# Attention feeding a gated MLP in fp32: S^T computed directly, the row maximum as a bias product, x^T divided by the sums

## The chip, the cores and the metric

The kernel runs on one core of a Trainium2 chip. The core has five engines that run side by side, each through its own list of instructions in order: TensorE (PE) multiplies, VectorE (DVE), ScalarE (ACT) and GpSimd (POOL) do elementwise work and reductions, and SyncE (SP) issues transfers. The metric is the device time of one execution in microseconds (us).

## The reference

The inputs are q, k and v of 8 batches, 8 heads, 576 positions and 64 numbers a head, and three weight matrices; all are fp32.

```python
scores = q @ k.transpose(0, 1, 3, 2) / sqrt(64)
mask = (pos[:, None] // 64) >= (pos[None, :] // 64)      # causal by blocks of 64
scores = where(mask, scores, -1e9)
attn = exp(scores - max(scores, -1))
attn = attn / (sum(attn, -1) + 1e-9)
x = (attn @ v) -> [8 * 576, 512]
out = (sigmoid(x @ w_gate) * (x @ w_val)) @ w_out        # 512 -> 1536 -> 512
```

The MLP's weights hold 1536 hidden features; the kernel counts them as 12 chunks of 128.

## The kernel before, in words

**Two ways of multiplying.** A product with fp32 operands is exact enough by itself, but it is issued as two matmul instructions and takes PE far longer for each column. The other way writes each operand as the sum of two parts of type float32r (names ending in H and L) and adds three products, H·H, L·H and H·L. The MLP uses the second way throughout.

**Pairs of heads.** The attention walks through 32 pairs p: 8 batches times 4 pairs of heads. Both heads of a pair lie in the 128 partitions, 64 rows each, and `tile_position` lets two matmuls with 64 rows work side by side. `load` (L206) fetches q, k and v of a pair, three pairs ahead for q and k. `prep(p)` (L266) turns k and q into K^T and Q^T: for p up to 4 by PE transposes and ACT, afterwards by DVE's 32x32 transposes (L274); for p from 8 on it also makes the H and L parts (L309 to L315), so that the scores of pairs 0 to 7 are fp32 products and those of pairs 8 to 31 are three float32r products, block 0 excepted.

**One pair's attention.** `attend(p)` (L331) returns a function that does one step of the pair at a time. Queries lie in blocks of 128 rows (3, 2, 1, 0) and a tail of 64; a block needs only the keys up to its own end.

- `s_blocks` and `s_tail` (L373, L393) compute S with queries on the partitions, write the mask with a DVE memset, take the negated row maximum with DVE (L367, L403), and let ACT write P = exp(S - max) with the row sums (L370, L405).
- `recip` and `norm` (L408, L412, with L480 for the tail) divide P by its sums: reciprocals and eight DVE multiplications, and one for the tail (ACT does three of these nine in pairs 4 to 7).
- `tr_main`, `tr_low`, `tr_tail` (L421, L430, L438) transpose P with 25 PE transposes, and ACT copies the results into G1 and G0 (L345).
- `av` (L449) computes x^T = V^T P^T in 14 fp32 products, 28 instructions; ACT copies it out of PSUM into `xT`.
- `finish` (L468) writes XH on ACT, stores `xT` to DRAM, and writes XL on POOL.

**The order.** The lists FIRST, REST and TURN (L30 to L34) give the steps of one iteration p of the loop at L777. Lower-case steps belong to pair p, and AV and TR to pair p-1; "k" and "q" run `prep(p+1)` and the loads of pair p+3. Behind each step stands a number of places, 12 in all in an iteration.

**The MLP between.** `mlp1` (L562) is a generator of PE work for the first 4 of the 12 chunks of hidden features: 192 matmuls of 288 columns (`hidden`, L121) and 48 or 60 of 512 columns (`out_mm`, L130) a batch. When a batch's fourth pair has had its AV, its generator is chained. At each place the loop deals about five of its matmuls (L799 to L811): they come behind the attention matmuls that were issued three places before (AHEAD) and, in the later pairs, behind the run of attention matmuls just ended. The contraction runs over pairs of heads in order, so a matmul of the fourth pair comes tenth to twelfth of twelve. KEEP (L23) holds back 52 or 32 matmuls for the change from one batch to the next. The elementwise work between the two products (`glu`, L141) is on ACT (tanh, cast), DVE (product) and POOL (low part).

**Other work in the same time.** `convert` (L73) rebuilds fp32 weights for the MLP on DVE and ACT, one piece for each of the first iterations (CONV_PLAN, L25). In the last two iterations `early_work` begins to prepare the second part.

**The second part.** Behind the loop, from L821 on, the other 8 chunks of hidden features are computed by seven products for each 2x2 block of the matrices (`product`, L831; `out_block`, L886). The change does not touch it.

**PSUM.** `ps_a` has three tiles of two banks, which the attention takes in turn; `ps_m` has two tiles of one bank for the MLP and for the first transposes.

## Time and profile before

| | us |
|---|---|
| three runs | 1222.08, 1225.13, 1223.28 |
| median of them | 1223.28 |
| span of the profiled execution | 1223.3 |
| first attention matmul | 7.40 |
| first matmul of AV of pair 0, and of pair 3 | 31.29, 79.09 |
| two batches in the steady stretch (252.00 to 400.10) | 148.10 |
| AV of the last pair | 597.08 |
| first matmul of the second part | 656.40 |

The profiled execution's span is 1223.3 us, the median of the runs to the digit shown, so differences worked out in the span carry over to the time. The profile gives for each engine the time in which it was busy. PE's instructions overlap in part, and a PE that is shown busy all the time is still only as fast as its instructions follow one another; so the cost of a PE instruction is read here from the distance between the starts of two that follow each other, not from its own duration. A row of the timeline gives the start, the length of the merged stretch, the engine, line and operation, what is written and read, and how many instructions were merged.

### The profile page before, as it was taken

What the parts mean: (1) busy time and instruction counts of PE and PEld (TensorE: products, weight loads), DVE (VectorE), ACT (ScalarE), POOL (GpSimd) and SP (SyncE); (2) the same over time, 40 slices, a digit from 0 to 9 for tenths busy, and PEclk for the clock granted to TensorE, in tenths of its full rate; (3) what the DMA queues carried; (4) which work ended last, traced back from release to release, by engine and by line L of the source; (5) the groups of instructions that cost most, each with busy time, mean ns of one, the idle gap of its engine ahead of it and who ended that gap; (6) DMA issues with size and microseconds to landing.
All of it is one profiled execution on the core that took longest, in us unless ns stands there. A gap on an engine that the chain in (4) does not pass through costs nothing.

```text
span 1223.3 us, 20662 instructions
## 1 busy us (share of the span) xinstructions
PE 1171.9 (96%) x7421; PEld 1030.8 (84%) x7421; DVE 861.9 (70%) x1691; ACT 651.2 (53%) x1523; POOL 337.9 (28%) x409
## 2 busy tenths in 40 slices
PE   6889899999999999999999999999999999999996
PEld 4567678888888888889798899999999998998995
DVE  6888876577575875757898967857866755755742
ACT  5778766666665776756544544444444322422420
POOL 1113232223222332313401132132132152361441
PEclk8889999999999999999999999999999999999998
DMA  8543242423424333332343245145197154264243
GB/s 212 130 103 90 53 109 43 113 68 63 109 60 102 70 76 85 76 86 82 97 147 128 62 160 190 41 166 187 37 326 289 55 180 140 77 197 136 79 148 103
DMA packets 239125, 142.91 MB, mean 117 GB/s; under 512 B 183600, under 2 KB 204080, under 8 KB 238384
## 3 DMA queue, kind: packets, MB, share of 16 engines
q1 hardware_dynamic: 227968, 122.43, 35.7%
q10 hardware_dynamic: 11056, 19.17, 4.4%
q8 instruction: 59, 0.97, 0.3%
q14 instruction: 42, 0.34, 0.1%
HBM read 94.37 MB, written 47.19 MB: 116 GB/s over the span
## 4 chain that ended last, share of the span: by engine, by line
PE 74%; DVE 14%; DMA 4%; ACT 4%; issue 2%; SPq 1%; POOL 1%; POOLq 0%; DVEq 0%; ACTq 0%
PE b L838 23%; PE bank L242 11%; PE m L126 11%; PE m L896 9%; PE m L135 7%; PE b L896 5%; PE bank L245 4%; DMA pr<-part_d 2%; DVE P L419 2%; ACT P L370 2%; DVE XL L730 2%; PE bank L126 1%; DVE nm L367 1%; PE bank L135 1%; DVE KQ L274 1%
## 5 line engine op out<-in xcount | busy, mean ns | idle before, releaser
L838 PE MATMUL b<-XH,w 128*128 128x384 f32 x1344 | 349.9, 336 | 5.4 <-DVE v L874 2.7
L838 PEld LDWEIGHTS b<-XH,w 128*128 128x128 f32 x1344 | 243.7, 188 | 12.6 <-DVE v L874 6.6
L838 PE MATMUL b<-XL,w 128*128 128x384 f32 x672 | 223.7, 335 | 0.0
L370 ACT ACTIVATE P<-bank,nm 128x512 f32<-128x512 f32 (+3 forms) x256 | 132.9, 533 | 86.4 <-DVE nm L367 74.7
L838 PEld LDWEIGHTS b<-XL,w 128*128 128x128 f32 x672 | 126.1, 188 | 1.2
L896 PE MATMUL m<-wo,hH 128*128 128x512 f32 x384 | 124.9, 391 | 0.0
L345 ACT COPY G<-bank 128x768 f32<-128x768 f32 (+3 forms) x160 | 106.2, 700 | 27.4 <-PE bank L245 26.0
L367 DVE TENSOR_REDUCE nm<-bank 128x2 f32<-128x1024 f32 (+3 forms) x128 | 104.8, 819 | 8.2 <-ACT P L370 5.7
L126 PE MATMUL m<-XH,wv 128*128 128x288 f32 x448 | 104.8, 304 | 2.9 <-DVE h L147 2.9
L126 PE MATMUL m<-XH,wg 128*128 128x288 f32 x448 | 106.1, 305 | 0.6 <-ACT t L145 0.6
L153 POOL TENSOR_TENSOR hL<-h,hH 128x288 fp32r<-128x288 f32 (+1 forms) x56 | 49.0, 875 | 182.4 <-ACT hH L152 171.7
L242 PE MATMUL bank<-G,VS 128*64 128x320 f32 (+4 forms) x896 | 95.2, 364 | 0.0
L245 PE MATMUL bank<-ident,P 128*128 128x128 f32 x640 | 90.0, 280 | 4.1 <-DVE P L419 3.6
L911 POOL TENSOR_TENSOR pr<-pr,pr 128x512 f32<-128x512 f32 x36 | 48.2, 1342 | 162.7 <-DMA pr<-part_d 117.0
L419 DVE TENSOR_SCALAR P<-P,sm 128x256 f32<-128x256 f32 (+3 forms) x248 | 87.8, 414 | 1.7
L242 PEld LDWEIGHTS bank<-G,VS 128*64 128x64 f32 x896 | 56.4, 138 | 36.8 <-issue 4.1
L245 PEld LDWEIGHTS bank<-ident,P 128*128 128x128 f32 x640 | 76.7, 144 | 12.4 <-ACT wo L117 3.1
L861 ACT ACTIVATE g<-g 128x384 f32<-128x384 f32 x72 | 37.2, 524 | 87.2 <-DVE g L874 62.2
L896 PEld LDWEIGHTS m<-wo,hH 128*128 128x128 f32 x384 | 71.9, 188 | 13.8
L729 ACT CAST XH<-XB 128x1536 fp32r<-128x1536 f32 (+2 forms) x72 | 65.9, 939 | 29.3 <-DVE XB L727 22.5
L473 POOL TENSOR_TENSOR XL<-xT,XH 128x576 fp32r<-128x576 f32 x32 | 47.2, 1476 | 123.5 <-ACT XH L470 107.8
L126 PEld LDWEIGHTS m<-XH,wv 128*128 128x128 f32 x448 | 74.8, 188 | 6.2 <-DVE h L147 4.2
(176 smaller groups left out, 2543.6 us busy)
## 6 DMA issues: line engine op xcount, KB each, us to landing
pr<-part_d SPq DMA_DIRECT2D x72, 256.0 KB, 3.7
xT_d<-xT ACTq DMA_DIRECT2D x32, 288.0 KB, 2.8
XB<-xT_d SPq DMA_DIRECT2D x16, 576.0 KB, 5.5
part_d<-ost SPq DMA_DIRECT2D x36, 256.0 KB, 4.0
out_dram<-ost SPq DMA_DIRECT2D x36, 256.0 KB, 2.8
VS<-in_v_dram SPq DMA_DIRECT2D x64, 128.0 KB, 2.5
part_d<-ost ACTq DMA_DIRECT2D x32, 256.0 KB, 2.1
rqk<-in_k_dram SPq DMA_DIRECT2D x108, 72.0 KB, 2.6
```

The source lines that it names most:

```text
L126: mm = nc.tensor.matmul(ps, lhsT=lh, rhs=rh, start=(i == 0), stop=(i == n - 1))
L135: mm = nc.tensor.matmul(ps, lhsT=lh[:, f, t * P:(t + 1) * P], rhs=rh, start=(i == 0), stop=(i == n - 1))
L153: lower.tensor_sub(out=hL, in0=h2[:, cols], in1=hH.bitcast(F32))
L242: pe_last[:] = [nc.tensor.matmul(*args, **kw).ins]
L245: pe_last[:] = [nc.tensor.transpose(*args).ins]
L345: mark("ACT", nc.scalar.copy(out=dst, in_=src))
L367: mark("DVE", nc.vector.tensor_reduce(out=nm[:, c0:c0 + 2], in_=ps[:, :, c:c + n], axis=AX.X, op=ALU.max, negate=True))
L370: mark("ACT", nc.scalar.activation(out=Pi[:, h], in_=ps[:, h, c:c + n], func=AF.Exp, bias=nm[:, c0 + h:c0 + h + 1], accum_out=sm[:, c0 + h ...
L419: mark("DVE", nc.vector.tensor_scalar_mul(Pi[:, h], Pi[:, h], sm[:, c0 + h:c0 + h + 1]))
L729: nc.scalar.copy(out=XO[j][0][:, a:b], in_=x)
L838: mm = nc.tensor.matmul(ps, lhsT=lh, rhs=rh, start=(first and k == 0), stop=(k == n - 1), skip_group_check=not first)
L896: mm = nc.tensor.matmul(po[t], lhsT=lh[:, f, t * P:(t + 1) * P], rhs=rh, start=(half == 0 and i == 0), stop=(half == 1 and i == 5))
```

## The change

- **The maximum is found ahead.** A new step generator `scores(p+1)` runs in iteration p. It computes S of the next pair with one product of the H parts, sets the mask, and has DVE write the negated row maxima into `NM`. Its step "m" transposes `NM` with five PE transposes, and ACT copies the result into `MT`.
- **S^T directly.** `weights` in `attend(p)` computes S^T, keys on the partitions, in four chunks (CHUNKS): three float32r products and a fourth product, `BL` by `MT`, that adds the row maximum (negated) and, for the masked half of a block, a very large negative number. ACT writes `PT[t] = exp` of a whole chunk, both heads in one instruction, without a bias and without sums.
- **No transposes and no division of P.** The 25 transposes of a pair, their copies into G1 and G0, the accumulator reads, `recip` and `norm` go. AV reads `PT` instead of G1 and G0.
- **The sums.** `add_up` adds the chunks' rows on POOL into `acc`, five additions; behind AV, six fp32 products with a 128x32 tile of ones, in four groups of 32 columns of PE, sum over the keys into PSUM.
- **The division.** `finish` copies x^T out of PSUM as before. DVE transposes the sums, adds 1e-9, takes nine reciprocals a row and transposes them back; SP stores the 4x288 result in DRAM and loads it again with two transfers that repeat it over 64 partitions each; DVE multiplies `xT` by it. XH, the store and XL come behind that.
- **H and L parts for every pair.** `prep` makes them for all pairs, from PSUM for p up to 4, and now runs two pairs ahead.
- **The order.** One list ORDER takes the place of the three; the steps of a group are one run of PE instructions, and the MLP matmuls that are dealt stand behind a run. The loop begins at p = -1. The MLP of a batch is chained in the group "add", after 7 places, instead of at AV.
- **At the start** POOL writes `NM`, `ones` and the mask pattern `Z`, and PE transposes `Z` into `BL`. `VSs` has two buffers instead of three; the buffer for w_out's pieces moves to another pool.

The diff, cut to its core:

```diff
-FIRST = (("s3", 1), ("TR2", 1), ("k", 1), ("s2", 1), ("TRt", 1), ("q", 1), ("t", 1), ("TRl", 1), ("sl", 1), ("AV", 2),
-         ("tr3", 1))
-REST = (("s", 3), ("t", 1), ("AV", 2), ("tr3", 1), ("k", 0), ("tr2", 1), ("q", 0), ("trl", 2), ("trt", 2))
-TURN = (("s3", 1), ("TR2", 1), ("k", 0), ("s2", 1), ("TRt", 1), ("q", 0), ("t", 1), ("TRl", 1), ("sl", 1), ("AV", 1),
-        ("tr3", 1), ("tr2", 1), ("trl", 1), ("trt", 1))
-N_FIRST = 7
+ORDER = ((("av", "0"), 3), (("s0", "1", "s1"), 2), (("2", "s2", "3"), 2), (("add", "mlp", "k", "q", "v"), 0), (("st",), 1),
+         (("prep",), 1), (("sm",), 1), (("prep",), 2))
+MASK, MASKED = -1e9, -1e30
...
+        PT = [at.tile([P, 2, n], F32, name=f"PT{n_}") for n_, n in enumerate((512, 320, 448, 320))]
...
+            H, Lo = (at.tile([P, 2, S], F32R, name=f"KQ{e}", bufs=2) for e in "HL")
...
+            def halves(i, cols, src):
+                if i:
+                    mark("ACT", nc.scalar.mul(out=H[:, 1, cols], in_=src, mul=scale))
+                else:
+                    mark("ACT", nc.scalar.copy(out=H[:, 0, cols], in_=src))
+                yield
+                hi = H[:, i, cols].bitcast(F32)
+                if i:
+                    mark("DVE", nc.vector.scalar_tensor_tensor(out=Lo[:, 1, cols], in0=src, scalar=scale, in1=hi,
+                                                               op0=ALU.mult, op1=ALU.subtract))
+                else:
+                    mark("DVE", nc.vector.tensor_sub(out=Lo[:, 0, cols], in0=src, in1=hi))
...
+        def scores(p):
+            (H, _), QB, NM = KQS[p], QBs[p % 2], NMs[p % 2]
+            def top(i, src):
+                mark("DVE", nc.vector.tensor_reduce(out=NM[:, i, :, 0], in_=src, axis=AX.X, op=ALU.max, negate=True))
+            def blocks(group):
+                ps = two_banks()
+                o = 0
+                for i in group:
+                    n = P * (i + 1)
+                    for h in range(2):
+                        matmul(ps[:, h, o:o + n], lhsT=H[rows(h), 1, i * P:(i + 1) * P], rhs=H[rows(h), 0, :n],
+                               start=True, stop=True, tile_position=(64 * h, 0))
+                    o += n
+                if len(group) == 1:
+                    nc.vector.memset(ps[0:64, :, o - 64:o], MASK)
+                else:
+                    nc.vector.memset(ps[0:64, :, 2 * P:].rearrange("p h (i n) -> p h i n", i=2)[:, :, :, 64:], MASK)
+                o = 0
+                for i in group:
+                    n = P * (i + 1)
+                    top(i, ps[:, :, o:o + n])
+                    o += n
+            def tail():
+                ps = two_banks()
+                for half in range(2):
+                    matmul(ps[:, half, :288], lhsT=QB.rearrange("p h q -> p (h q)"),
+                           rhs=H[:, 0, 288 * half:288 * half + 288], start=True, stop=True)
+                mark("DVE", nc.vector.tensor_reduce(out=NM[:, 4, 0, 0:1], in_=ps[:, :, :288], axis=AX.XY, op=ALU.max,
+                                                    negate=True))
+                mark("DVE", nc.vector.tensor_copy(out=NM[:, 4, 1, 0:1], in_=NM[:, 4, 0, 0:1]))
+            def turn():
+                MT = at.tile([P, S], F32R, name="MT")
+                ps = two_banks()
+                for i in range(4):
+                    transpose(ps[:, 0, i * P:(i + 1) * P], NM[:, i].rearrange("p h x -> p (h x)"), ident)
+                transpose(ps[:, 1, :P], NM[:, 4].rearrange("p h x -> p (h x)"), ident)
+                mark("ACT", nc.scalar.copy(out=MT[:, :4 * P], in_=ps[:, 0]))
                 for h in range(2):
+                    mark("ACT", nc.scalar.copy(out=MT[rows(h), 4 * P:], in_=ps[rows(h), 1, 64 * h:64 * h + 64]))
+                state[p] = MT
+            return lambda what: {"0": lambda: blocks((3,)), "1": lambda: blocks((2, 0)), "2": lambda: blocks((1,)),
+                                 "t": tail, "m": turn}[what]()
+        CHUNKS = (((0, 256, 320), (3, 384, 192)), ((0, 0, 256), (4, 512, 64)), ((1, 128, 448),), ((2, 256, 320),))
...
+            H, Lo = KQS.pop(p)
+            MT, VS = state.pop(p), VSs[p % 2]
+            def weights(t):
                 ps = two_banks()
+                o = 0
+                for c, q0, w in CHUNKS[t]:
+                    k0 = c * P if c < 4 else S - P
+                    ops = [(x[:, 0, k0:k0 + P], y[:, 1, q0:q0 + w]) for x, y in ((H, H), (Lo, H), (H, Lo))]
+                    ops.append((BL[:, c], MT[:, q0:q0 + w]))
+                    for j, (x, y) in enumerate(ops):
+                        for h in range(2):
+                            matmul(ps[:, h, o:o + w], lhsT=x[rows(h)], rhs=y[rows(h)], start=(j == 0),
+                                   stop=(j == len(ops) - 1), tile_position=(64 * h, 0))
+                    o += w
+                mark("ACT", nc.scalar.activation(out=PT[t], in_=ps[:, :, :o], func=AF.Exp))
+            def add_up():
+                acc = at.tile([P, 2, S - P], F32, name="acc")
+                add = nc.gpsimd.tensor_add
+                add(out=acc[:, :, :P], in0=PT[1][:, :, P:2 * P], in1=PT[2][:, :, :P])
+                add(out=acc[:, :, P:], in0=PT[0][:, :, :320], in1=PT[2][:, :, P:])
+                add(out=acc[:, :, P:], in0=acc[:, :, P:], in1=PT[3])
+                add(out=acc[:, :, 2 * P:], in0=acc[:, :, 2 * P:], in1=PT[0][:, :, 320:])
+                add(out=acc[:, :, 3 * P:], in0=acc[:, :, 3 * P:], in1=PT[1][:, :, 2 * P:])
+                state[p] = acc
+            def values():
+                acc = state.pop(p)
                 pv = two_banks()
+                for i, pieces in enumerate((
+                        ((0, PT[0], 0, 0, 320), (1, PT[2], P, 0, 320), (2, PT[3], 0, 0, 320), (4, PT[1], 256, 256, 64),
+                         (3, PT[0], 320, P, 192)),
+                        ((0, PT[1], 0, 0, 256), (1, PT[2], 0, P, P)))):
+                    for j, (c, G, go, oo, w) in enumerate(pieces):
                         for h in range(2):
                             matmul(pv[rows(h), i, oo:oo + w], lhsT=VS[:, c, rows(h)], rhs=G[:, h, go:go + w],
                                    start=(j == 0), stop=(j == len(pieces) - 1), tile_position=(0, 64 * h))
+                us = two_banks()
+                for half, oo, G, go, w in ((0, 0, PT[1], 0, P), (1, 0, acc, 160, 288), (0, P, acc, 0, 160)):
+                    for h in range(2):
+                        r = 64 * h + 32 * half
+                        matmul(us[r:r + 32, 0, oo:oo + w], lhsT=ones, rhs=G[:, h, go:go + w], start=True, stop=True,
+                               tile_position=(0, r))
+                return pv, us
+            def finish(pv, us):
+                xT = at.tile([P, S], F32, name="xT", bufs=2)
+                T = at.tile([P, 288], F32, name="T")
+                r9 = at.tile([P, 9], F32, name="r9")
                 for i, (n, q0) in enumerate(((320, 256), (256, 0))):
+                    mark("ACT", nc.scalar.copy(out=xT[:, q0:q0 + n], in_=pv[:, i, :n]))
+                nc.vector.transpose(out=T, in_=us[:, 0, :288])
+                nc.vector.tensor_scalar_add(r9, T[:, ::32], 1e-9)
+                nc.vector.reciprocal(r9, r9)
+                mark("DVE", nc.vector.transpose(out=T.rearrange("p (b c) -> p b c", c=32),
+                                                in_=r9.unsqueeze(2).to_broadcast([P, 9, 32])))
+                r_d = dram.tile([4, 288], F32, name="r_d", bufs=2)
+                nc.sync.dma_start(out=r_d, in_=T[::32])
+                rb = at.tile([P, S], F32, name="rb")
+                for h in range(2):
+                    nc.sync.dma_start(out=rb[rows(h)],
+                                      in_=r_d[2 * h:2 * h + 2].rearrange("a n -> (a n)").partition_broadcast(64))
                 XH, XL = x_tiles(b)
+                nc.vector.tensor_mul(out=xT, in0=xT, in1=rb)
                 nc.scalar.copy(out=XH[:, hp], in_=xT)
+                nc.scalar.dma_start(out=xT_d[b, hp * P:(hp + 1) * P, :], in_=xT)
                 nc.gpsimd.tensor_sub(out=XL[:, hp], in0=xT, in1=XH[:, hp].bitcast(F32))
...
+        for c in range(5):
+            ps = mbank()
+            transpose(ps[:, :P], Z[:, c], ident)
+            nc.scalar.copy(out=BL[:, c], in_=ps[:, :P])
...
+        now = prev = None
+        for p in range(-1, n + 1):
+            if p >= 0:
+                early_work(p, 0)
+            prev, now = now, attend(p) if 0 <= p < n else None
+            nxt = scores(p + 1) if p + 1 < n else None
+            pr = prep(p + 2) if 0 <= p + 2 < n else iter(())
             tick = 0
...
+            for group, places in ORDER:
+                run_begins()
+                for what in group:
+                    if what == "av":
+                        if prev:
+                            prev("av")
+                    elif what == "mlp":
+                        if p > 0 and pairs[p - 1][1] == NP - 1:
+                            pb = pairs[p - 1][0]
+                            mlp = itertools.chain(mlp, mlp1(pb, mbank if p < n else bank))
+                            left += F1 * 48 * NC // 4 + 3 * F1 * (5 if pb % 2 else 4)
+                            rate = (left - KEEP[pb > 0]) / (4 * TICKS)
+                    elif what == "prep":
+                        next(pr, None)
+                    elif what in "kq":
+                        if 0 <= p and p + 3 < n:
+                            load(p + 3, what)
+                    elif what == "v":
+                        if 0 < p and p + 1 < n:
+                            load(p + 1, "v")
+                    elif what[0] == "s":
+                        if nxt:
+                            nxt(what[1])
+                    elif now:
+                        now(what)
+                run_ends()
...
```

More of the change, by code (lines that the diff above doesn't have):

```diff
@@ L247, in transpose, with run_begins, run_ends @@
                 behind(pe_last[0], hold[0])
+        def run_begins():
+            opening[:] = dealt[-1:]
+        def run_ends():
+            hold[:] = pe_last
         def two_banks():
@@ L750, in attn_glu_kernel @@
         load(1, "v")
-        load(2, "v")
-        prev = None
         mlp = iter(())
```

301 lines of the change are left out of this document (58 added, 243 removed).

## The prediction

> **What bounds the kernel now.** I read the page first, then busy time by stretch, then PE's timeline where PE is full, then the groups by line.
>
> ```profile
> PE 1171.9 (96%) x7421; PEld 1030.8 (84%) x7421; DVE 861.9 (70%) x1691; ACT 651.2 (53%) x1523; POOL 337.9 (28%) x409
> PE 74%; DVE 14%; DMA 4%; ACT 4%; issue 2%; SPq 1%; POOL 1%; POOLq 0%; DVEq 0%; ACTq 0%
> ```
>
> ```profile
> 7.40:75.00 67.60, 52.18 (x307) 33.27 (x308) 56.67 (x125) 48.87 (x135) 9.37 (x14) 0.87 0.65 154
> 75.00:105.00 30.00, 29.42 (x211) 22.50 (x209) 23.04 (x52) 23.71 (x60) 8.87 (x11) 0.96 0.40 90
> 105.00:174.00 69.00, 61.95 (x431) 49.58 (x431) 58.01 (x122) 51.12 (x135) 19.51 (x25) 0.98 0.33 79
> 252.00:400.10 148.10, 147.31 (x1143) 127.45 (x1144) 101.04 (x216) 100.77 (x275) 43.80 (x72) 1.00 0.36 81
> 548.20:700.00 151.80, 144.33 (x938) 128.98 (x938) 137.00 (x278) 80.07 (x179) 29.96 (x30) 0.99 0.31 99
> ```
>
> The columns are the stretch, its length, busy time of PE, PEld, DVE, ACT and POOL, the granted clock, the DMA share and GB/s. There are three regimes. From 252 to 400 PE is busy 147.3 of 148.1 us while DVE and ACT have a third free: there only PE's own work counts. From 7.4 to 75, before any MLP work exists, PE is idle for 15.4 us and DVE is busy 84%: the attention runs at the pace of DVE and its round trips. From 105 to 174 PE is idle for 7.1 us. The change takes work from ACT and DVE, which are not the bound where most of the pairs run; so its worth is PE's sum per pair, plus what becomes of the idle time at the start, plus new waits.
>
> **PE's work for a pair, steady.** Start distances give the prices.
>
> ```profile
> 400.04 2.93 PE L242 MATMUL bank<-G,VS 128*64 128x320 f32 x28
> 402.89 0.40 PE L126 MATMUL m<-XL,wg 128*128 128x288 f32 x1
> ...
> 404.07 0.29 PE L126 MATMUL m<-XH,wv 128*128 128x288 f32 x1
> 404.20 0.29 PE L126 MATMUL m<-XL,wv 128*128 128x288 f32 x1
> 404.33 1.03 PE L245 MATMUL bank<-ident,P 128*128 128x128 f32 x8
> 405.12 0.51 PE L126 MATMUL m<-XH,wv 128*128 128x288 f32 x2
> ...
> 411.14 0.50 PE L242 MATMUL bank<-KH,QH 64*128 64x512 f32 x2
> 411.47 0.40 PE L242 MATMUL bank<-KH,QL 64*128 64x512 f32 x2
> 411.70 0.40 PE L242 MATMUL bank<-KL,QH 64*128 64x512 f32 x2
> 411.94 0.34 PE L242 MATMUL bank<-KH,QH 64*128 64x384 f32 x2
> ...
> 412.59 0.28 PE L242 MATMUL bank<-KH,QL 64*128 64x256 f32 x2
> 412.70 0.28 PE L242 MATMUL bank<-KL,QH 64*128 64x256 f32 x2
> 412.82 0.39 PE L242 MATMUL bank<-KQ 64*128 64x128 f32 x4
> 413.14 0.53 PE L126 MATMUL m<-XH,wv 128*128 128x288 f32 x2
> ...
> 415.37 0.33 PE L242 MATMUL bank<-KH,QBH 128*128 128x288 f32 x1
> ...
> 416.20 0.30 PE L126 MATMUL m<-XH,wv 128*128 128x288 f32 x1
> ```
>
> ```profile
> 400.04:416.83 16.79, 9.65 (x61) 8.23 (x60) 1.00 0.35 72
> ```
>
> The last row counts the MLP's matmuls (L126) from one AV to the next: 60, and 0.13 us from start to start makes 8.0 us. The other 8.8 us of the 16.79 are attention: AV 2.85, transposes 0.79 for eight, so 2.45 for 25, the block scores 2.0, the tail 0.83, which makes 8.1; 0.7 is left for about ten changes between kinds (0.07 each).
>
> What goes: 2.45 (transposes) and 2.83 (scores).
>
> What comes:
> - The maximum's pass. A float32r pair of matmuls costs 0.235 us at 512 columns and 0.115 at 256, so 0.457 ns a column. 512+384+256 columns make 0.53; block 0 has 128, between 0.06 (by columns) and 0.1 (one transposed tile's weights), taken as 0.09; the tail is two of the six, 0.28. Sum 0.90.
> - S^T. The chunks are 320, 192, 256, 64, 448 and 320 columns, 1600 in all, times four products: 6400 x 0.457 ns = 2.92. The 64-column pieces by columns are 0.03 a pair; two weight loads can't be hidden behind that. A 256-column pair hides two in 0.115, a transpose needs 0.1 with its own. I take 0.1 for each of the four, so +0.28 (0 to 0.35): 3.2.
> - Five transposes of NM: 0.5.
> - The sums: 576 fp32 columns for each head. AV has 1600 columns in 2.85, 1.78 ns a column with two heads side by side: 1.03. If the four groups of 32 columns run side by side, the 288-column pieces decide: 0.52. I take 0.8, between the ends, since the row shows two side by side and not four. The Trainium skill, "TensorE: Matmul & The Clock Gate", section "Why this matters for your kernels", says that small outputs at distinct groups of 32 columns run at the same time; by it the term would be 0.52, and no row here shows four.
> - Changes between kinds: runs are fewer (five for seven), about 0.5.
>
> After: 2.85 + 0.9 + 3.2 + 0.5 + 0.8 + 0.5 = 8.75, against 8.8: **no gain on PE**, -0.05 a pair (-0.4 to +0.3). 24 pairs make -1 (-10 to +7). In pairs 4 to 7 the old scores are fp32, 1856 columns x 1.78 ns = 3.3 for 2.83: four times 0.5, -2. The same in pairs 0 to 3 is hidden behind DVE.
>
> **DVE, ACT and POOL for a pair.**
>
> ```profile
> L370 ACT ACTIVATION_READ_ACCUMULATOR P<-bank,nm 128x1 f32 x256 | 53.5, 209 | 0.0
> L345 ACT COPY G<-bank 128x768 f32<-128x768 f32 x64 | 50.5, 803 | 10.4 <-PE bank L245 10.3
> L367 DVE TENSOR_REDUCE nm<-bank 128x2 f32<-128x1024 f32 x32 | 39.0, 1220 | 0.8
> L419 DVE TENSOR_SCALAR P<-P,sm 128x512 f32<-128x512 f32 (+3 forms) x32 | 10.1, 377 | 0.1
> L313 DVE TENSOR_TENSOR KL<-KQ,KH 128x576 fp32r<-128x576 f32 x24 | 19.3, 803 | 1.7 <-ACT KH L309 0.4
> L153 POOL TENSOR_TENSOR hL<-h,hH 128x224 fp32r<-128x224 f32 x28 | 19.9, 712 | 60.5 <-ACT hH L152 50.2 <-ACT hHt L152 9.4
> L473 POOL TENSOR_TENSOR XL<-xT,XH 128x576 fp32r<-128x576 f32 x32 | 47.2, 1476 | 123.5 <-ACT XH L470 107.8 <-issue 15.6
> xT_d<-xT ACTq DMA_DIRECT2D x32, 288.0 KB, 2.8
> VS<-in_v_dram SPq DMA_DIRECT2D x32, 32.0 KB, 2.1
> ```
>
> ACT loses its accumulator reads (53.5/32 = 1.7 us a pair) and the copies into G (the 768-wide alone 1.6), and gains about 1 for MT. POOL gains five additions of 256, 640, 640, 384 and 128 columns. Between POOL's 224 columns (0.71) and 576 (1.48) lie 2.2 ns a column, so 0.2 + 2.2 ns x columns: 0.8 + 1.6 + 1.6 + 1.0 + 0.5 = 5.5 us. DVE at the start: the normalisation (eight at 0.38 = 3.0, the tail 0.5) and 0.8 of reciprocals go; the low parts (two of the 0.8 kind) and the division come. The division is two transposes of 288 columns (half of a 576 transpose, 0.4 each), two short operations at 0.2, and a 576 product at 0.75: 2.0. So 4.3 go and 3.7 come: DVE's pace at the start is nearly what it was.
>
> **The start.**
>
> ```profile
> 31.29 2.93 PE L242 MATMUL bank<-G,VS 128*64 128x320 f32 x28
> 46.78 2.93 PE L242 MATMUL bank<-G,VS 128*64 128x320 f32 x28
> 61.02 2.93 PE L242 MATMUL bank<-G,VS 128*64 128x320 f32 x28
> 79.09 1.30 PE L242 MATMUL bank<-G,VS 128*64 128x320 f32 x8
> ```
>
> These are AV of pairs 0 to 3, 16 us apart, of which DVE is busy 84%. A deeper look-ahead may raise that share, but prep two pairs and scores one pair ahead are DVE work (about 8 us) that now stands before AV of pair 3. I leave AV of pair 3 at 78 to 79. Its x^T comes later: sums 0.8, DVE 1.2, a store (2.1, the 32 KB row) and a load (2.8, the 288 KB row), the product 0.75: about 8 us before XH and XL, and the MLP's first batch waits with its fourth quarter. PE meanwhile has S^T of pair 4 and scores of pair 5 (4.1 us). Net **+4** (-6, if DVE is filled better, to +12). From 105 to 174 the idle 7.1 us shrinks, since ACT loses 5 us in a pair there: **-3** (-7 to 0). In later batches the same latency is covered: the MLP is chained seven places behind AV, and KEEP holds 32 matmuls, 4.3 us, beyond that. At the end of the loop the covering work is w_out's 48 or more matmuls; +1 (0 to +5).
>
> **New waits in the steady part.** The first run is AV, sums, S^T chunk 0, in one piece, so nothing can be dealt into a wait inside it. The three tiles of ps_a turn eleven times in a pair for nine; the closest is chunk 3, which needs the tile that DVE's reductions of blocks 2 and 0 release: S of block 3 to there is about 3.8 us of PE, DVE's two memsets and three reductions 3.0. Behind DVE's product, which waits for the load, those reductions wait too. I take 0.15 us a pair, **+4** (0 to +10). What it costs beyond that is the first rival.
>
> Sum: 1223.3 - 1 - 2 + 4 - 3 + 1 + 4 = **1226**. The span is the median of the runs to the digit, so no correction is added. The parts' ends give 1219 to 1234 for this case, taken together less than their plain sum since they are independent.
>
> **Rivals.**
> - *The sums come late (slower).* POOL's additions can end only behind the exponential of chunk 3, and the six products behind AV need them. From the end of chunk 2's matmuls to the sums there are 9.2 us of PE in an iteration of 288-column matmuls (0.7 of run 3, seven places of 0.67, 0.8 of tail and transposes, AV 2.85 and changes); the exponential takes 1.3 of it. POOL has 5.5 for the additions, 1.5 for XL and about 1.1 for casts of h, 8.1 for 7.9, and QB's copies besides. It decides from the point where POOL's 8 us exceed that window. One us in each of 28 pairs is +28, less 3 that is in the forecast: 1251 (1234 to 1270). For it: POOL works in order and is held by waits for ACT today. Against it: POOL is busy only 43.8 of 148.1 us, and in iterations with 512-column matmuls a place is longer.
> - *The additions hold DVE.*
>
> ```profile
> L480 DVE TENSOR_SCALAR Pt<-Pt,sm x28: 504/937/1732, 18.9 to 590.5; 128x576 f32<-128x576 f32 x28
> 274.08 1.72 DVE L480 TENSOR_SCALAR Pt<-Pt,sm 128x576 f32<-128x576 f32 x1
> 274.06 1.42 POOL L473 TENSOR_TENSOR XL<-xT,XH 128x576 fp32r<-128x576 f32 x1 [4.61 <-ACT XH L470]
> ```
>
>   The tail's multiplication takes 0.5 alone and 1.72 beside XL: DVE stood while POOL worked. With 5.5 us more of POOL in a pair of 18.5, three DVE operations on SBUF (two low parts, the product) would each meet one in three times, at about 1.2: 1.2 us of DVE a pair. It decides where reductions are late for chunk 3; 0.3 of it on PE, 24 times: 1233. By the Trainium skill, "SBUF — State Buffer", section "SBUF: two separate sides", DVE and GpSimd take a shared port as an exclusive lock for a whole instruction; these rows agree.
> - *The relief counts (faster).* If the deeper look-ahead fills PE at the start (half of the 15.4 us), the 7.1 us go, the sums run four side by side (-0.3 x 28) and no new wait appears: 1223.3 - 7 - 5 - 8 + 6 (latency) = 1210 (1198 to 1219). For it: ACT and DVE fall everywhere. Against it: DVE is as full at the start as before.
>
> **How the numbers follow.** The forecast has 0.41, the late sums 0.23, the held DVE 0.08, the relief 0.28. The forecast is the likeliest, 1226, with its own range 1219 to 1234. About 0.3% (3.7 us) is what a measurement of this kernel can tell from no change. Of the forecast's 0.41, 0.03 lies below 1219.6, 0.23 within, 0.15 above 1227. So faster 0.31, same 0.23, slower 0.46. The range cuts about a tenth at each side: 1206 to 1252.
>
> **What would show it.** PE: AV to AV in an iteration of 60 matmuls again 16.5 to 17.1 us. Idle: PE before the MLP's first matmul about 5 us more than now, and less from 105 to 174. First rival: PE's matmuls with `ones` with idle time before them, ended by POOL. Second: L480's successor, the product with rb, well over 0.8 us. I am wrong if S^T costs more than 3.4 us in the timeline, or the sums differ from 0.5 to 1.0, or PE in the steady batches is busy less than 98%.

## The result: 7.3% slower, far outside the range

| | before | after |
|---|---|---|
| median of four runs | 1223.26 us (1222.08 to 1225.13) | 1313.22 us (1312.12 to 1314.12) |
| span of the profiled execution | 1223.3 | 1310.0 |
| first matmul of AV of pair 8 | 173.9 | 198.1 |
| eight AVs later in the steady part | 148.1 | 168.6 |
| first matmul of AV of the last pair | 597.0 | 684.3 |
| from there to the end | 626.3 | 625.8 |

The ratio is 1.073, with an interval of 1.0713 to 1.0748. The forecast was 1226 with a range of 1206 to 1252. The last row of the table says that nothing was lost in the second part; the other rows say where the 86.7 us of span came from: 24.2 up to AV of pair 8, and 63 in the 23 pairs between that and the last AV. (The last AV before the change starts at 597.01; the 597.08 in the table ahead of the prediction is off by 0.07.)

First the head of the page of the changed kernel: busy time by engine, and the chain of work that ended last.

```profile
PE 1215.5 (93%) x8194; PEld 1054.3 (80%) x8194; DVE 832.2 (64%) x1504; ACT 533.1 (41%) x1010; POOL 475.5 (36%) x512
PE 66%; DVE 14%; DMA 10%; issue 4%; ACT 2%; SPq 1%; POOL 1%; DVEq 0%; POOLq 0%; ACTq 0%
```

ACT and DVE have become lighter, as meant, and POOL busier. PE is busy for 44 us more, and its share has fallen to 93% all the same. In the chain DMA has gone from 4% to 10%: a transfer now ends waits that decide the end.

The busy time by stretch shows in which regime. The columns are those of the prediction: the stretch, its length, PE, PEld, DVE, ACT, POOL, the granted clock, the DMA share and GB/s.

```profile
7.40:75.00 67.60, 52.56 (x398) 37.95 (x396) 49.00 (x94) 28.30 (x60) 22.66 (x27) 0.82 0.53 129
75.00:105.00 30.00, 21.23 (x147) 14.91 (x146) 23.04 (x42) 11.83 (x20) 12.78 (x12) 0.72 0.48 120
105.00:174.00 69.00, 56.16 (x466) 43.94 (x466) 56.60 (x97) 33.43 (x68) 34.53 (x36) 0.95 0.37 89
252.00:400.00 148.00, 138.04 (x1156) 113.50 (x1156) 75.76 (x139) 62.52 (x127) 65.83 (x77) 0.99 0.36 86
402.20:404.80 2.60, 2.60 (x12) 2.55 (x11) 0.02 (x1) 0.70 (x1) 2.52 (x3) 0.50 0.00 0
405.60:409.50 3.90, 3.90 (x31) 3.72 (x30) 3.15 (x6) 2.37 (x8) 2.40 (x5) 1.00 0.22 36
```

In the steady stretch from 252 to 400, where PE had no time to lose, it is idle for 10.0 of 148 us: 93% busy, under the 98% that the prediction named as a sign of being wrong. From 75 to 105 it is idle for 8.8 us where it had been busy 29.4 of 30, and from 105 to 174 for 12.8 instead of 7.1.

**One iteration, followed through its queues.** In PE's timeline of the changed kernel, AV of a pair begins at 409.92. A row is the start, the length, the engine, line and operation, and how many were merged; what stands in brackets is the idle time before it and what ended that.

```profile
409.92 2.93 PE L253 MATMUL bank<-PT,VS 128*64 128x320 f32 x28
...
417.96 0.48 PE L253 MATMUL bank<-KQH 64*128 64x384 f32 x4
...
420.95 0.28 PE L253 MATMUL bank<-KQH 64*128 64x256 f32 x2
423.05 0.41 PE L253 MATMUL bank<-KQH 64*128 64x320 f32 x2 [1.82 <-DVE NM L343]
```

The last row is S^T chunk 3 (320 columns). It comes directly behind the scores of block 1 (256 columns), and PE stands for 1.8 us before it. What it waits for is a reduction on DVE (NM, L343), since that releases the PSUM tile that chunk 3 writes. This is DVE's timeline beside it:

```profile
414.52 0.48 DVE L453 STREAM_TRANSPOSE T<-r 128x288 f32<-128x288 f32 x1
417.45 0.17 DVE L355 MEMSET bank<- 64x128 f32 x1 [2.45 <-PE bank L253]
417.65 1.23 DVE L343 TENSOR_REDUCE NM<-bank 128x2 f32<-128x1024 f32 x1
420.51 0.76 DVE L462 TENSOR_TENSOR xT<-xT,rb 128x576 f32<-128x576 f32 x1 [1.63 <-DMA rb<-r_d]
421.31 0.27 DVE L357 MEMSET bank<- 64x256 f32 x1
421.62 1.29 DVE L343 TENSOR_REDUCE NM<-bank 128x2 f32<-128x768 f32 x2
```

and SP's:

```profile
415.03 0.53 SPq L456 DMA_DIRECT2D r_d<-T  x1
416.71 1.10 SPq L459 DMA_DIRECT2D rb<-r_d  x2
```

Read together: T, the transposed reciprocals, is ready at 415.0. Its store is issued at 415.03 and the load at 416.71, and the product with rb starts at 420.51, 5.5 us after T. From 418.88 to 420.51 DVE does nothing at all, though the scores of blocks 2 and 0 are in PSUM (PE's row at 417.96): the product stands at the head of DVE's queue, and the memset and the reductions stand behind it. They end at 422.91, and chunk 3 starts at 423.05. So the wait for the transfer passes from DVE to PE, through a PSUM tile that has nothing to do with the division.

**The price of the waits.** Eight pairs from AV to AV, by stretch, in the changed kernel,

```profile
283.93:452.57 168.64, 156.62 (x1317) 129.49 (x1316) 87.23 (x160) 71.99 (x145) 76.75 (x88) 0.98 0.36 86
```

are the same work on PE as eight pairs of kernel 2 below, which has no such wait: 1317 matmuls in 168.6 us against 1318 in 151.8. The difference of 16.8 us is 2.1 a pair. Of this PE's waits, as the profile sums them for the changed kernel over those eight pairs (total, times, longest), are 12.0:

```profile
PE bank L253 <- DVE NM L343: 12.0, 7, 2.1
```

Another part is the clock. In PE's timeline of the changed kernel, chunk 3 of the pair before the one above waited just as long, and what follows is slower:

```profile
401.45 0.42 PE L253 MATMUL bank<-KQH 64*128 64x320 f32 x2 [1.80 <-DVE NM L343]
402.65 0.44 PE L123 MATMUL m<-XL,wv 128*128 128x288 f32 x1
402.89 0.68 PE L123 MATMUL m<-XH,wv 128*128 128x288 f32 x2
```

The MLP's matmuls start 0.24 us apart here, where the prediction counted 0.13. The last two of the rows by stretch have the reason: a granted clock of 0.50 from 402.2 to 404.8, and 1.00 again from 405.6. Slice by slice the clock fell so after two of the seven waits, each time for some 3 us, which is 3.4 us lost; after the wait at 423.05, no shorter, it did not fall. 12.0 and 3.4 leave 1.4 of the 16.8 unexplained.

The same waits from 252 to 550, for a comparison below, are these for PE,

```profile
PE bank L253 <- DVE NM L343: 20.4, 14, 2.5
```

for DVE,

```profile
DVE xT L462 <- DMA rb<-r_d: 20.2, 14, 2.2
```

and for ACT:

```profile
ACT XH L463 <- DVE xT L462: 32.0, 14, 3.6
```

The cast XH on ACT waits for the product, and the next exponential stands behind it in ACT's queue. At the start of the kernel, where no MLP work lies between, PE waits through that second queue. ACT at 64 us:

```profile
63.84 0.67 ACT L463 CAST XH<-xT 128x576 fp32r<-128x576 f32 x1 [6.20 <-DVE xT L462]
64.41 0.70 ACT L409 ACTIVATE PT<-bank 128x640 f32<-128x640 f32 x1
```

and PE, whose AV of pair 2 waits for that exponential:

```profile
65.16 5.17 PE L253 MATMUL bank<-PT,VS 128*64 128x320 f32 x22 [4.06 <-ACT PT L409]
```

### The profile page after: what moved, and what is told of

The parts are those of the page before. It is cut to its first block, busy times and chain, and to the rows that moved or that the text cites. A ratio compares the mean times of both kernels' runs of the same rounds, so it can differ in the third digit from the quotient of the medians.

```text
span 1310.0 us, 21761 instructions
## 1 busy us (share of the span) xinstructions
PE 1215.5 (93%) x8194; PEld 1054.3 (80%) x8194; DVE 832.2 (64%) x1504; ACT 533.1 (41%) x1010; POOL 475.5 (36%) x512
## 4 chain that ended last, share of the span: by engine, by line
PE 66%; DVE 14%; DMA 10%; issue 4%; ACT 2%; SPq 1%; POOL 1%; DVEq 0%; POOLq 0%; ACTq 0%
PE b L800 22%; PE bank L253 14%; PE m L123 9%; PE m L858 9%; DMA rb<-r_d 5%; PE m L132 5%; PE b L858 5%; DMA r_d<-T 3%; DVE NM L343 2%; DMA pr<-part_d 1%; DVE XL L680 1%; PE bank L258 1%; PE bank L132 1%; SPq L459 1%; DVE T L450 1%
## 5 line engine op out<-in xcount | busy, mean ns | idle before, releaser
L253 PE MATMUL bank<-KQH 64*128 64x256 f32 (+7 forms) x640 | 104.6, 352 | 56.9 <-DVE NM L343 49.4
L409 ACT ACTIVATE PT<-bank 128x640 f32<-128x640 f32 (+2 forms) x128 | 106.2, 836 | 89.3 <-PE bank L253 84.7
L253 PEld LDWEIGHTS bank<-KQH 64*128 64x128 f32 x640 | 59.4, 192 | 88.0 <-issue 68.9
L253 PE MATMUL bank<-PT,VS 128*64 128x320 f32 (+4 forms) x896 | 103.7, 379 | 8.3 <-ACT PT L409 8.3
L343 DVE TENSOR_REDUCE NM<-bank 128x2 f32<-128x1024 f32 (+3 forms) x128 | 102.2, 819 | 2.9
L253 PEld LDWEIGHTS bank<-PT,VS 128*64 128x64 f32 x896 | 60.0, 144 | 49.3 <-issue 11.4
L123 PEld LDWEIGHTS m<-XH,wg 128*128 128x128 f32 x448 | 79.1, 198 | 4.1 <-issue 1.7
L666 POOL TENSOR_TENSOR XB<-XB 128x384 f32<-128x384 f32 x20 | 26.4, 1322 | 145.2 <-DMA XB<-xT_d 122.6
L680 DVE TENSOR_TENSOR XL<-XB,XH 128x1536 fp32r<-128x1536 f32 (+2 forms) x72 | 77.6, 1083 | 0.9 <-ACT XH L679 0.4
L858 PE MATMUL m<-wo,hL 128*128 128x512 f32 x192 | 75.2, 392 | 0.0
```

Of the source, the lines that this page charges most:

```text
L123: mm = nc.tensor.matmul(ps, lhsT=lh, rhs=rh, start=(i == 0), stop=(i == n - 1))
L253: pe_last[:] = [nc.tensor.matmul(*args, **kw).ins]
L343: mark("DVE", nc.vector.tensor_reduce(out=NM[:, i, :, 0], in_=src, axis=AX.X, op=ALU.max, negate=True))
L409: mark("ACT", nc.scalar.activation(out=PT[t], in_=ps[:, :, :o], func=AF.Exp))
L666: t1 = eng.tensor_sub(out=XB[:, 4], in0=XB[:, 1], in1=XB[:, 0])
L680: sub = nc.vector.tensor_sub(out=XO[j][1][:, a:b], in0=x, in1=XO[j][0][:, a:b].bitcast(F32))
```

## The experiments

The theory after this reading: the waits of the product and of XH for the two transfers, in the in-order queues of DVE and ACT, are most of the loss (A). The rivals: POOL's additions hold DVE through the kernel, or come late for the sums (B); PE's own work for a pair is larger than the prediction's sum (C). Each short diff is against the changed kernel. Kernels 1, 5 and 6 were timed four times each; kernels 2, 3, 4, 7 and 8 once, while the four times of kernel 1 lie 5.1 us apart, so a few us of a single time mean little. Kernels 2, 3, 7 and 8 leave out something that the output needs and serve only to price it. Kernels 1 to 3 and the fifth shared one set of runs of the kernel before (median 1222.80), the other four another (1221.89). "Steady" below is the time of eight pairs, from one AV to the eighth after it, in the stretch from 250 to 460: 148.1 before (251.94 to 400.04), 168.6 after (283.93 to 452.57).

| kernel | us | steady, 8 pairs | AV of pair 8 at |
|---|---|---|---|
| before | 1223.3 | 148.1 | 173.9 |
| after | 1313.2 | 168.6 | 198.1 |
| 1 product issued later | 1269.2 | 155.2 | 192.1 |
| 2 constant in place of rb | 1254.8 | 151.8 | 184.9 |
| 3 no additions | 1306.7 | 170.1 | 192.9 |
| 4 product on POOL | 1284.9 | 158.0 | 198.8 |
| 5 reciprocal of all 576 columns | 1290.9 | 156.1 | 194.9 |
| 6 sums spread by PE, no transfers | 1266.4 | 154.0 | 182.4 |
| 7 as 2, no bias product | 1237.5 | 147.7 | 176.6 |
| 8 as 2, no additions | 1244.9 | 151.2 | 177.3 |

**1. The product issued later.** Product, XH, the store of x^T and XL move behind the last reduction, into the group of the additions.

```diff
-ORDER = (..., (("add", "mlp", "k", "q", "v"), 0), ...
+ORDER = (..., (("div", "add", "mlp", "k", "q", "v"), 0), ...
...
+                state["div", p] = lambda: divide(xT, rb)
+            def divide(xT, rb):
...
-                nc.vector.tensor_mul(out=xT, in0=xT, in1=rb)
+                behind(nc.vector.tensor_mul(out=xT, in0=xT, in1=rb).ins, last["DVE"])
```

> The division's product, XH, the store and XL are issued in the group "add", behind the reductions of block 1, instead of right behind the two transfers. Theory A (the product waits on DVE for the transfers, and XH on ACT, with the reductions and exponentials that free PSUM tiles queued behind them): PE's idle time in the steady stretch, 10 of 148 us, falls below 2, a pair takes 1.5 to 2.2 us less, and the start gains too; 1245 to 1265 us. Theory B (POOL's additions hold DVE or come late): the waits stay, 1300 to 1315 us. Theory C (PE's own work per pair has grown, idle time is a by-product): at most 15 us less, 1298 us or more.

It took 1269.2 us, a ratio of 1.0389 (1.0369 to 1.0409): 44 us came back by order alone, with the same instructions and the same transfers. The steady stretch of this kernel:

```profile
252.00:400.00 148.00, 147.23 (x1261) 120.09 (x1259) 83.32 (x150) 66.24 (x133) 74.83 (x83) 1.00 0.39 93
```

PE is busy for 147.2 of 148 us again, and no wait of PE for NM is left from 252 to 550. The time is 4 us over what A expected. Eight pairs take 3.4 us more than in kernel 2. XL now stands in the additions' window, and PE waits for the sums from 252 to 550, 0.9 us in three places; besides, in most pairs the sums come in two pieces, of 0.34 and 0.61 us, where the changed kernel has one of 0.62 in nearly all. The start has got back 6.0 of its 24.2 us (AV of pair 8 at 192.1): ACT still stands before XH in the first three pairs, for 3.2, 5.5 and 4.7 us, against 3.7, 6.2 and 5.3 in the changed kernel.

**2. A constant in place of rb.** x^T is multiplied by a tile of ones; the loads of rb are gone, the store of r_d and all other work stay.

```diff
+        rb = at.tile([P, S], F32, name="rb")
+        nc.gpsimd.memset(rb, 1.0)
...
-                rb = at.tile([P, S], F32, name="rb")
-                for h in range(2):
-                    nc.sync.dma_start(out=rb[rows(h)], ...)
```

> x^T is multiplied by a constant tile of ones instead of the reciprocals of the sums; the reciprocals are still made and stored, but not loaded again, so the product is there without its wait. Theory A: as much as or more than moving it, 1240 to 1262 us. Theory B: 1300 us or more, since the additions are untouched. Theory C: 1298 us or more.

It took 1254.8, 58 us less. This kernel leaves out the wait and also the transfers that it waits for; kernel 1 keeps the transfers and gets 44 of the 58 back, so at least that much comes from where the wait stands. The rows of this kernel for the stretch of round trips and the steady one:

```profile
105.00:174.00 69.00, 56.98 (x486) 45.36 (x482) 63.99 (x106) 33.58 (x68) 31.60 (x35) 0.95 0.31 71
252.00:400.00 148.00, 147.97 (x1285) 123.50 (x1284) 84.94 (x157) 69.85 (x142) 75.63 (x85) 1.00 0.36 79
```

From 252 to 400 PE is never idle, and still eight pairs take 151.8 us, 3.7 more than before: 0.47 us a pair more are PE's own work (C), no wait. From 105 to 174 PE remains idle for 12.0 us.

**3. No additions.** POOL adds nothing; the sums read a constant tile.

```diff
-                acc = at.tile([P, 2, S - P], F32, name="acc")
-                add = nc.gpsimd.tensor_add
-                add(...)
-                state[p] = acc
+                state[p] = acc_c
```

> The five additions on POOL are left out and the sums are taken over a constant tile. Theory A: within 5 us of the changed kernel, 1308 to 1318 us, because the transfers and the product's wait stay. Theory B: 30 us less or more, below 1285 us. Theory C: no change.

1306.7, 6.5 us less than after and 1.3 below what A expected; AV of pair 8 is 5.2 us earlier, and the steady part is no shorter (170.1). PE's wait from 252 to 550 in this kernel is as long as with the additions (20.4); its lines are numbered two higher, for what was added above:

```profile
PE bank L255 <- DVE NM L345: 21.1, 15, 2.3
```

B is out as the cause of the steady loss.

**4. The product on POOL.** This frees DVE's queue and leaves ACT's as it is.

```diff
-                nc.vector.tensor_mul(out=xT, in0=xT, in1=rb)
+                nc.gpsimd.tensor_mul(out=xT, in0=xT, in1=rb)
```

> The product of x^T with the reciprocals is on POOL, at the same place in the program; XH on ACT still comes behind it. If DVE's queue is what holds the PSUM tiles (the releaser that the trace names in the steady stretch): PE's idle time from 252 to 400 falls below 3 us, 1250 to 1278 us, with the start not much better, since ACT's exponential still stands behind XH there. If ACT's queue does it: PE's idle time stays above 6 us with ACT as the releaser, 1285 to 1310 us.

1284.9: 28 us back, half of what kernel 2 gets. AV of pair 8 is at 198.8, no earlier than in the changed kernel, as expected for a start where ACT's exponential still stands behind XH. PE's wait for NM is gone from 252 to 550, so it did come through DVE's queue; but the steady part is 6.2 us longer than in kernel 2. This is the steady stretch of this kernel:

```profile
252.00:400.00 148.00, 144.25 (x1218) 118.19 (x1218) 78.87 (x140) 65.97 (x138) 84.76 (x92) 1.00 0.38 90
```

and these are its waits on ACT and POOL from 252 to 550:

```profile
ACT XH L463 <- POOL xT L462: 45.6, 15, 4.7
POOL xT L462 <- DMA rb<-r_d: 93.4, 15, 12.2
```

PE is idle for 3.75 us. XH waits longer than before the move, with the exponentials behind it. The result lies between the two expectations. It shows that freeing DVE alone isn't enough; it does not divide the rest cleanly between ACT's queue and POOL's, which now waits as well.

**5. The reciprocal of all columns.** The ones are 64 columns wide, so PE's sums land on all 64 partitions of a head, DVE takes the reciprocal of 576 columns from PSUM, and there are no transfers. The 1e-9 is not added.

```diff
-        ones = at.tile([P, 32], F32, name="ones")
+        ones = at.tile([P, 64], F32, name="ones")
...
-                nc.vector.transpose(out=T, in_=us[:, 0, :288])
...
+                mark("DVE", nc.vector.reciprocal(rb.rearrange("p (a n) -> p a n", a=2), us[:, :, :288]))
```

> The tile of ones has 64 columns, so PE leaves the sums on all 64 partitions of a head; DVE takes the reciprocals straight from there (1e-9 is not added) and multiplies, with no transposes of the sums and no transfers. Theory A: as without the wait, plus about 0.4 us of PE a pair for sums that run two side by side instead of four: 1245 to 1270 us. Theory B: 1300 us or more. Theory C: 1313 us or more, since PE's work grows by 0.4 us a pair.

1290.9, a ratio of 1.0563 (1.0546 to 1.0581), a miss of 21 us. The group by line says why:

```profile
L448 DVE RECIPROCAL rb<-bank 128x576 f32<-128x576 f32 x32 | 120.2, 3756 | 95.0 <-PE bank L253 95.0
```

The reciprocal takes 3.76 us of DVE itself, where the changed kernel has 5.5 us from T to the product, and DVE is where the reductions queue. The kernel says nothing against A, but is no test of it.

**6. Sums spread by PE, few reciprocals.** As 5, but DVE transposes the two halves, takes 18 reciprocals and transposes back. It computes all that the changed kernel does, without transfers.

```diff
+                r18 = at.tile([P, 18], F32, name="r18")
+                for half in range(2):
+                    nc.vector.transpose(out=rb[:, 288 * half:288 * half + 288], in_=us[:, half, :288])
+                nc.vector.tensor_scalar_add(r18, rb[:, ::32], 1e-9)
+                nc.vector.reciprocal(r18, r18)
+                mark("DVE", nc.vector.transpose(out=rb.rearrange("p (b c) -> p b c", c=32),
+                                                in_=r18.unsqueeze(2).to_broadcast([P, 18, 32])))
```

> As with the 64-column tile of ones, but the reciprocals are taken of 18 numbers a row between two transposes of 576 columns on DVE, so nothing waits for a transfer and no long reciprocal is needed. Waits theory (product's wait, then PE's work): the constant factor's 1255 us plus 0.4 us of PE in 27 pairs or so: 1258 to 1272 us, and AV of pair 8 at 182 to 192. If the transfers were harmless and only the product's place mattered: as with the later product, 1269 us.

1266.4, a ratio of 1.0361 (1.0334 to 1.0389), as expected. The time alone doesn't tell it from kernel 1, whose four runs overlap with its own; AV of pair 8 at 182.4, against 192.1 there, does, and says that at the start the transfers still cost when the product is issued later. Its sums, in two groups of 64 columns, take 1.07 us (286.20 to 287.27). It has the lowest median of the versions that compute the whole, and is 3.6% slower than the kernel before.

**7. As 2, without the bias product.** Neither the mask nor the maximum is added to S^T: three products instead of four.

```diff
-                    ops.append((BL[:, c], MT[:, q0:q0 + w]))
```

> As e2_factor_const (constant factor), and the bias product of S^T is left out, so neither mask nor maximum is added. If PE's work is what is left between e2_factor_const and the kernel before: 6400 becomes 4800 columns, 0.73 to 0.85 us a pair less in the steady 24 pairs, a batch-pair period (8 pairs) of 145 to 146.5 us instead of 151.9, and 1230 to 1238 us in all. If it is not: within 5 us of 1255.

1237.5, in the expected interval, but in part by luck: eight pairs take 147.7 where 145 to 146.5 was expected, 0.52 us a pair less than kernel 2, and 8.3 of the 17.4 us come before AV of pair 8, where none was counted. A quarter of S^T's measured 3.65 us (below) would be 0.91 a pair. Why the step is smaller is open.

**8. As 2, without the additions.** The wait and the additions both left out.

> As e2_factor_const, and POOL's five additions are left out. If POOL's additions stretch DVE's work at the start (the weight conversion's 128x512 operations take 1.05 us there instead of 0.42): AV of pair 8 comes 5 to 12 us earlier than 184.8, and 1240 to 1250 us. If they don't: 1250 to 1257 us. In the steady stretch nothing changes (151 to 152 us for 8 pairs).

1244.9: 9.9 us less than kernel 2, 7.5 of them up to AV of pair 8. The rows of DVE's conversion of weights (L103, L106 in both) from 7.4 to 174 show how the additions reach DVE. In the changed kernel:

```profile
L106 DVE SCALAR_TENSOR_TENSOR cgv<-cgv 128x512 uint32<-128x512 uint32 x8 | 9.0, 1120 | 0.1
L103 DVE TENSOR_SCALAR cgv<-cgv 128x512 uint32<-128x512 uint32 x8 | 8.4, 1049 | 0.0
```

In kernel 8:

```profile
L106 DVE SCALAR_TENSOR_TENSOR cgv<-cgv 128x512 uint32<-128x512 uint32 x8 | 5.6, 695 | 0.1
L103 DVE TENSOR_SCALAR cgv<-cgv 128x512 uint32<-128x512 uint32 x8 | 3.2, 402 | 0.0
```

These two kernels differ by the wait too, but two closer pairs, which differ by the additions alone, say the same: 1120 and 1049 ns in the changed kernel against 691 and 420 in kernel 3, and 916 and 777 in kernel 2 against 695 and 402 in kernel 8. From 105 to 174 PE of kernel 8 is busy for 61.93 of 69 us, as before the change (61.95):

```profile
105.00:174.00 69.00, 61.93 (x535) 51.86 (x535) 60.43 (x118) 37.72 (x74) 17.51 (x22) 0.95 0.34 79
```

**The account of the 86.7 us of span.** Kernel 2 against after gives the wait, kernel 8 against kernel 2 the additions, and kernel 8 against before the rest, each cut at AV of pair 8 and at the last AV:

| | up to AV of pair 8 | to the last AV | to the end | sum |
|---|---|---|---|---|
| wait for the division | 13.2 | 43.4 | 0.4 | 57.0 |
| POOL's additions | 7.5 | 3.4 | -1.0 | 9.9 |
| rest | 3.4 | 16.2 | 0.1 | 19.8 |

The parts depend on the order in which they are taken out: with the wait in place the additions are worth 5.3 us of span (kernel 3 against after), without it 9.9. The rest is in good part PE's own work: by kernel 8's steady eight pairs (151.2 against 148.1) 0.39 us a pair, 9 us for 23 pairs. The remaining 7.2 of the 16.2, in pairs outside the eight measured, and the 3.4 up to AV of pair 8 stay unexplained. Kernel 8, with both the wait and the additions left out, still takes 1244.9 us. Whether another order of the same work could win that back, at the start say, where PE is idle, is not shown.

## Why the prediction was wrong

**The step that failed: "New waits in the steady part", taken at 0.15 us a pair, +4.** The runs show about 2.1 us a pair there ((168.6 - 151.8)/8), and 43 us between AV of pair 8 and the last AV. The prediction had the mechanism in words: chunk 3 needs the tile that the reductions of blocks 2 and 0 release, and "Behind DVE's product, which waits for the load, those reductions wait too". But its price came from comparing PE's 3.8 us with DVE's 3.0 of work, which leaves the waiting out, and the sentence about the load got no price of its own. Its own terms would have given one. From the start of AV: AV 2.85, sums 0.8, DVE 1.2, store 2.1, load 2.8 and product 0.75 make 10.5 us. The reductions of blocks 2 and 0 with their memset are the 3.0 less block 3's 1.2 and its memset of 0.2, so the tile is free at 12.1. Measured, the product ends at 11.4 (421.27 - 409.92) and the tile is free at 13.0. PE gets to chunk 3 at 11.3 (423.05 less the 1.82 idle, less 409.92). So the predicted terms, held against PE's measured 11.3, give a wait of 0.8 us a pair; it measured 1.8 here, and with what follows it, 2.1 a pair on average. The tile came 0.9 us later than these terms say, and 0.6 of that is the way through DRAM: 5.5 us from T to the product, where 2.1 and 2.8 were added.

**PE's work for a pair: no gain, as said, but a loss of 0.47 instead of the -0.05 forecast.** The terms can be read from PE's timeline of kernel 2, in an iteration of 60 MLP matmuls from AV at 435.49 to AV at 452.83:

```profile
435.49 2.93 PE L255 MATMUL bank<-PT,VS 128*64 128x320 f32 x28
438.35 0.30 PE L255 MATMUL bank<-PT,ones 128*32 128x128 f32 x2
...
438.97 0.41 PE L255 MATMUL bank<-KQH 64*128 64x320 f32 x2
439.23 0.31 PE L255 MATMUL bank<-KQH,KQL 64*128 64x320 f32 x2
439.37 0.31 PE L255 MATMUL bank<-KQL,KQH 64*128 64x320 f32 x2
...
440.19 0.53 PE L123 MATMUL m<-XH,wg 128*128 128x288 f32 x2
...
442.36 0.63 PE L255 MATMUL bank<-KQH 64*128 64x512 f32 x4
...
443.17 0.20 PE L255 MATMUL bank<-KQH 64*128 64x64 f32 x2
443.20 0.28 PE L255 MATMUL bank<-KQH,KQL 64*128 64x64 f32 x2
...
443.54 0.48 PE L255 MATMUL bank<-KQH 64*128 64x384 f32 x4
443.95 0.53 PE L123 MATMUL m<-XH,wv 128*128 128x288 f32 x2
...
445.48 0.47 PE L255 MATMUL bank<-KQH 64*128 64x448 f32 x2
...
447.18 0.40 PE L123 MATMUL m<-XH,wg 128*128 128x288 f32 x1
```

AV is 2.86 (2.85 forecast). The sums take 0.62, from 438.35 to 438.97, between the 0.52 of four groups of 32 columns side by side and 1.03 of two: most of them run together, as the Trainium skill, "TensorE: Matmul & The Clock Gate", section "Why this matters for your kernels", says. The five transposes of NM take 0.38 (0.5 forecast). The term that was too small is S^T with the maximum's pass: their runs take 1.22 (from 438.97), 1.59 (from 442.36) and 1.70 (from 445.48), and the tail 0.27, which makes 4.78 where 0.9 + 3.2 were forecast. S^T alone is 3.65 of it by the starts of its matmuls, above the 3.4 named as the point where the sum is wrong. The 64-column pieces are not the reason: the four pairs take 0.37 together, from 443.17 to 443.54, where 0.4 was estimated. What the prices of these two left out is the edges of a run: the first pair of 320 columns takes about 0.25 us until the next one starts, the second 0.14. The stretches of the MLP, with the changes around them, take 8.69, as before the change (8.70), where the forecast has 8.0 and 0.5. The differences add up to 0.58 in this iteration, 0.47 on average over the eight pairs, and AV to AV is 17.3 us where 16.5 to 17.1 was the mark. That the new products eat up what the transposes and the old scores leave was right; the size was off by half a microsecond.

**The start: +4, -3 and -2 forecast, +24 measured up to AV of pair 8.** AV of pair 3, left at 78 to 79, starts at 86.8, and at 77.1 in kernel 2. Up to pair 8, kernel 2 gives 13.2 us to the wait and kernel 8 another 7.5 to the additions. "About 8 us before XH and XL" was counted once, as a delay of the MLP's first batch. But XH stands in ACT's queue ahead of the exponentials of the next pair, so each of the first pairs waits (6.2 us on ACT, 4.1 on PE at 65), not only the fourth. ACT's 5 us less work was to shrink PE's idle time from 105 to 174 (-3). It grew by 5.8 us instead. With the wait gone it was still 12.0, without the additions 10.2 (kernel 3), and it is back at the old 7.1 only with both gone.

**Rival 1, late sums**, was given 0.23 and didn't come: PE has no wait for acc from 252 to 550 in the changed kernel, and leaving the additions out gains 6.5 us, none of it there. POOL's estimate held. The two largest of the five additions in the groups of the changed kernel are

```profile
L415 POOL TENSOR_TENSOR acc<-PT,PT 128x640 f32<-128x640 f32 x32 | 50.7, 1584 | 0.0
L416 POOL TENSOR_TENSOR acc<-acc,PT 128x640 f32<-128x640 f32 x32 | 50.6, 1582 | 3.2 <-ACT PT L409 1.9
```

and with the others (36.2, 23.9 and 20.5 us in 32 pairs) they make 5.7 us a pair for 5.5. **Rival 2, the additions hold DVE**, is true, with a price of 9.9 us where 7 was named (0.3 in each of 24 pairs), but three quarters of it fall up to AV of pair 8, where the conversions of weights stretch, and little on the steady pairs that it counted. Its own sign didn't show: the product with rb has a median of 0.76 us, where the forecast counted 0.75. By the Trainium skill, "SBUF — State Buffer", section "SBUF: two separate sides", some DVE operations and those of GpSimd hold a shared pair of ports as an exclusive lock for a whole instruction; the 402 and 1049 ns agree with it. **Rival 3, the relief**, fell with the idle time at the start.

## What to carry to other kernels

An instruction that waits for a transfer holds everything behind it on its engine: list what is queued there, and work out from the chain's own terms when each of it is due, above all what frees a PSUM tile; then issue the waiting instruction behind that (44 of the 90 us came back so here). Compare times of readiness along a chain, not sums of work: 3.0 us of DVE's work against 3.8 of PE's said nothing while DVE stood. A kernel full on one engine gains nothing from work taken off the others, if the new form puts half a microsecond a pair onto that one.

## What the runs showed of the hardware

- A reciprocal of 128x576 from PSUM took DVE 3756 ns, where one of 128x9 took 210. Taken on the transposed sums, where few columns hold them all, it is cheap.
- After some of PE's waits of 1.8 us the granted clock was 0.50 for about 3 us, with matmuls 0.24 us apart instead of 0.13; after others as long it stayed at 1.00. What decides was not found.
- From four ready rows of 288 numbers in SBUF through DRAM to the first use of the copy spread over 128 partitions were 5.5 us in the iteration shown: 1.7 from the store's issue to the load's, and 3.8 from there to the product.
- In a kernel with POOL's additions a 128x512 DVE operation with one tensor input took 1049 ns on average, 402 in one without them, and one with two 1120 and 695.
- Of four pairs of matmuls with 64 moving columns (64-row operands, two heads) in a row the first took 0.03 us and the others 0.11 each, about what the prediction read for 256 columns (0.115).
